# Transposing DMAs in place of TensorE transposes, and 111 instead of 105 tiles of the softmax on VectorE

## The chip, the cores and the metric

The kernel runs on one core of a Trainium2 chip. That core has a matrix engine (TensorE, "PE" in the profile), a vector engine (VectorE, "DVE"), a scalar engine that evaluates the exponential (ScalarE, "ACT"), a general engine (GpSimd, "POOL"), and a sequencer that mostly issues transfers (SyncE, "SP"). The engines run in parallel, each through its own list of instructions in a fixed order, and wait for one another through semaphores. An instruction that waits holds everything behind it on the same engine. The metric is the device time of one execution in microseconds (us); less is better.

## The reference

One input `x` of 2048 tokens by 512 features goes through two attention branches of 32 heads of width 16, and a gate per token mixes the two outputs:

```python
g = sigmoid((x * gate_w).sum(-1, keepdims=True))
# A: ordinary attention, no mask
q, k, v = heads(x @ A_wqkv)
a = concat(softmax(q @ k.T * 16 ** -0.5) @ v) @ A_wo
# B: linear attention with a learned feature map
q, k, v = heads(x @ B_wqkv)
phi = lambda u: concat(softmax(u @ w_phi), softmax(-u @ w_phi))   # 16 + 16 features
kv, z = phi(k).T @ v, phi(k).sum(tokens)
b = concat((phi(q) @ kv) / (phi(q) @ z + 1e-6)) @ B_wo
return g * a + (1 - g) * b
```

Everything that goes in or out is bfloat16. Branch A costs most by far: 32 heads times 2048 x 2048 scores, each of which needs an exponential.

## The kernel before

**Branch A.** The scores are cut into 2048 units of 128 keys by 512 queries. Four units (four heads, same keys and queries) make a pack, 16 packs (all keys) a group, and there are 32 groups: four chunks of 512 queries times eight groups of four heads. For a unit TensorE computes the scores (`_scores`, line 839), and most units get their exponential on ScalarE (`_exp`, line 891), three or two units in one instruction by turns, from a ring of five PSUM banks. The exponentiated tile then is the moving operand of the product with V (`_values`, line 958), and after the 16th pack of a group VectorE transposes and normalises the sums (`_norm`, lines 979 to 995).

**Packs away.** Some packs get their exponential on VectorE instead. `_vector_bits` (line 777, four instructions a pack) turns the scores into the bits of a bfloat16 power of two, and `_vector_terms` (line 795, three instructions a pack) makes three shifted copies. TensorE adds four such tiles with weights instead of one, so a pack away costs twelve more products. `PACKS` says how many packs of each group go away, `CHOICE` at which of the places 1, 4, 7, 10, 13 in the group: 105 packs in all.

**Branch B** is spread between the packs. `_b_fuse` folds `w_phi` into the weights of k and of q: it transposes a quarter of `WB` by TensorE against the identity (line 1050), copies it out of PSUM (line 1055), multiplies (line 1068, name `wphi`) and copies back (line 1073). `_b_pair` makes the features of two tiles of 128 tokens, with the exponential on ScalarE (line 1124). For queries, `_b_phit` transposes the features (TensorE line 1189, VectorE line 1196), `_b_num` forms numerator and denominator, divides, and transposes the result (lines 1235 and 1241), and `_b_out` multiplies by `WoB`. `_out` adds branch A's product, copies out of PSUM and stores.

**The start.** `x` is loaded in five pieces as it lies in memory and turned by TensorE (`_x_transpose`, line 609) and a copy on VectorE (line 615) into `xT`, the features on the partitions. The projections read `xT`. SP issues, in this order: the five pieces of `x`, three later parts of `A_wqkv`, `gate_w`, `B_wqkv`, the 32 small blocks of `w_phi`, the two output weights, and from then on only the stores.

**What sets the order.** A list scheduler in the kernel (`Plan.order`) writes the order of every engine at build time, by an account of costs and latencies written in the code (for instance 0.45 us of SP for each small transfer in `_shared_dma`, 0.5 for another one), by due times in packs (`prio`, `K0`, `SK`, `Q0`, `SQ`), release times (`rel`) and free PSUM banks. The order is then fixed: if a transfer lands later than that account has it, the engine waits at the instruction that needs it, however much other work stands behind. Scores have the first priority on TensorE, but they stand in the same single list.

## Time and profile before

| | us |
|---|---|
| median of three runs (lowest, highest) | 791.22 (790.95, 792.47) |
| time of the profiled execution | 790.92 |
| its span, which the trace covers | 788.9 |
| ScalarE busy | 768.6 |
| TensorE busy, as modelled | 766.6 |
| VectorE busy | 729.4 |

All three compute engines are busy for more than nine tenths of the span. The trace gives a start and an end to every instruction and tells what released it when its engine had been idle. A row of the table of instructions has the source line, the engine and operation, output and input tiles with shapes, the count, the total and mean time, and the idle time ahead of it with its cause. A row of the timeline has start, duration, engine and instruction; `SPq` is SP issuing a transfer, and the row covers the issuing alone, not the transfer.

### The profile page before, as it was taken

To read this page: it belongs to the slowest core of one execution; us is meant where nothing else is said; L and a number is where in the kernel's file an instruction comes from. 1 tells how busy PE (TensorE), PEld (TensorE's weight loads), DVE (VectorE), ACT (ScalarE), POOL (GpSimd) and SP (SyncE) were. 2 spreads that over 40 slices of the span, in tenths; PEclk is the share of its full clock that TensorE was granted. 3 is DMA by queue.
4 is the path that set the end of the run, shared out by engine and by line. 5 is a ranking of instruction groups with operands and counts; after the bars stand their busy time and mean duration, and the time that the engine had idled before them with its cause. 6 is when DMAs were issued, how large, how long until landed. Compare 5 with 4: busy or idle time off the path is not lost.

```text
span 788.9 us, 17147 instructions
## 1 busy us (share of the span) xinstructions
PE 766.6 (97%) x7506; PEld 243.9 (31%) x7506; DVE 729.4 (92%) x1325; ACT 768.6 (97%) x671; POOL 6.9 (1%) x14
## 2 busy tenths in 40 slices
PE   9999999999999999999999999999999999999998
PEld 4333333233222232222222333223332233223332
DVE  5778989898999999999999999899988999799994
ACT  5799999999999999999999999999999999999996
POOL 2000000000000000000000000000000000000000
PEclk9999999999999999999999999999999999999999
DMA  9200000000000000000000000000000000000000
GB/s 267 55 2 1 2 1 2 1 2 1 2 1 2 1 2 1 2 2 1 2 2 1 2 1 8 15 8 1 2 7 21 2 2 2 14 15 1 2 2 27
DMA packets 10857, 9.48 MB, mean 12 GB/s; under 512 B 3616, under 2 KB 10272, under 8 KB 10784
## 3 DMA queue, kind: packets, MB, share of 16 engines
q1 hardware_dynamic: 8912, 7.75, 3.2%
q8 instruction: 58, 0.95, 0.5%
q10 hardware_dynamic: 1872, 0.66, 0.3%
q14 instruction: 15, 0.12, 0.1%
HBM read 6.31 MB, written 2.10 MB: 11 GB/s over the span
## 4 chain that ended last, share of the span: by engine, by line
ACT 81%; DVE 9%; PE 9%; issue 0%
ACT ET L891 78%; ACT bq L1124 3%; DVE va L777 3%; PE ps L839 3%; DVE vp L795 2%; PE ps L958 2%; PE ps L634 1%; PE ps L688 1%; PE ps L1252 1%; PE ps L1285 0%; PE ps L594 0%; PE ps L965 0%; PE ps L609 0%; DVE xT L615 0%; DVE VB L1083 0%; DVE bq L1121 0%
## 5 line engine op out<-in xcount | busy, mean ns | idle before, releaser
L891 ACT ACTIVATE ET<-ps 128x1536 bf16<-128x1536 f32 (+1 forms) x651 | 740.5, 1327 | 11.4 <-PE ps L839 10.4
L839 PE MATMUL ps<-qT,kT 32*128 32x512 bf16 x2048 | 340.2, 384 | 12.7 <-ACT ET L891 8.7
L777 DVE TENSOR_SCALAR va<-ps 128x512 uint16<-128x512 f32 x420 | 276.5, 682 | 6.7 <-PE ps L839 5.9
L795 DVE TENSOR_SCALAR vp<-va 128x2048 uint16<-128x2048 uint16 x315 | 209.0, 686 | 1.3 <-PE ps L958 0.9
L839 PEld LDWEIGHTS ps<-qT,kT 32*128 32x128 bf16 x2048 | 83.9, 91 | 266.6 <-ACT ET L891 145.3
L958 PE MATMUL ps<-ET,V 128*32 128x512 bf16 x1628 | 158.4, 386 | 0.6 <-DVE T L979 0.3
L958 PE MATMUL ps<-vp,vc 128*32 128x512 bf16 x840 | 74.8, 384 | 0.9 <-DVE vp L795 0.9
L965 PE MATMUL ps<-kT,zero 128*32 128x512 bf16 x832 | 75.0, 386 | 0.0
L958 PEld LDWEIGHTS ps<-ET,V 128*32 128x32 bf16 x1628 | 41.3, 94 | 68.8 <-issue 57.0
L634 PE MATMUL ps<-WB,xT 128*128 128x512 bf16 x192 | 54.8, 383 | 0.6 <-DVE T L979 0.2
L958 PE MATMUL ps<-vp,V 128*32 128x512 bf16 x420 | 41.3, 384 | 0.9 <-DVE vp L795 0.9
L958 PE MATMUL ps<-va,V 128*32 128x512 bf16 x420 | 41.7, 387 | 0.0
L634 PE MATMUL ps<-xT,WA 128*128 128x512 bf16 (+1 forms) x132 | 36.8, 377 | 0.4 <-DVE va L777 0.2
L1124 ACT ACTIVATE bq<-bq 128x2048 bf16<-128x2048 bf16 x16 | 31.7, 1983 | 0.0
L958 PEld LDWEIGHTS ps<-vp,vc 128*32 128x32 bf16 x840 | 19.8, 95 | 34.3 <-issue 17.0
L965 PEld LDWEIGHTS ps<-kT,zero 128*32 128x32 bf16 x832 | 18.6, 94 | 36.2 <-issue 34.2
L979 DVE STREAM_TRANSPOSE T<-ps 128x512 f32<-128x512 f32 x32 | 22.7, 708 | 7.4 <-PE ps L958 7.3
L1099 DVE CAST bq<-ps 128x512 bf16<-128x512 f32 x32 | 21.8, 683 | 6.6 <-PE ps L634 6.6
L674 DVE TENSOR_TENSOR qT<-ps,mask 128x1024 bf16<-128x1024 f32 x15 | 18.3, 1217 | 2.8 <-PE ps L634 2.8
L634 PEld LDWEIGHTS ps<-WB,xT 128*128 128x128 bf16 x192 | 12.6, 97 | 24.8 <-issue 12.0
L1294 DVE CAST WB<-ps 128x512 bf16<-128x512 f32 x12 | 8.3, 690 | 12.6 <-PE ps L1285 11.2
L688 PE MATMUL ps<-WA,xT 128*128 128x128 bf16 x256 | 19.6, 220 | 0.0
(84 smaller groups left out, 439.6 us busy)
## 6 DMA issues: line engine op xcount, KB each, us to landing
xn<-in_A_x_dram SPq DMA_DIRECT2D x3, 512.0 KB, 7.1
WB<-in_B_wqkv_dram SPq DMA_DIRECT2D x1, 1536.0 KB, 8.8
out_dram<-WB SPq DMA_DIRECT2D x12, 128.0 KB, 1.7
WA<-in_A_wqkv_dram SPq DMA_DIRECT2D x3, 384.0 KB, 8.8
xn<-in_A_x_dram SPq DMA_DIRECT2D x2, 256.0 KB, 3.7
wphi<-in_B_w_phi_dram SPq DMA_DIRECT2D x32, 0.5 KB, 2.1
WoA<-in_A_wo_dram SPq DMA_DIRECT2D x1, 512.0 KB, 4.1
WoB<-in_B_wo_dram SPq DMA_DIRECT2D x1, 512.0 KB, 5.1
```

What stands on the lines that cost most here:

```text
L634: ins = e.matmul(self._bank(job)[:, 0:n], lhs(c), rhs(c), start=(c == 0), stop=(c == 3))
L674: [lambda e, b: e.tensor_tensor(self.qT[:, s0:s0 + 2, :], b[:, None, :].to_broadcast([P, 2, QCH]), self.mask[:, :, None].to_broadcast([P, ...
L688: ins = e.matmul(self._bank(job)[:, P * tt:P * tt + P], self.xT[:, c, QCH * j + TOK * tt:QCH * j + TOK * tt + TOK], self.WA[:, 2, c, P * c ...
L777: parts.append(op("DVE", lambda e, j=j, job=job: e.tensor_scalar(self.va[:, slot, j, :], self._bank(job), SCALE * LOG2E * 128.0, (127.0 - ...
L795: self.plan.op("DVE", lambda e, t=t, shift=shift: e.tensor_scalar(flat(t), a, float(shift), None, op0=ALU.add), 0.07 + n * 0.00026, reads= ...
L839: return e.matmul(out, self.kT[32 * i:32 * i + 32, cp, kt * TOK:(kt + 1) * TOK], self.qT[32 * i:32 * i + 32, s, :], start=True, stop=True, ...
L891: o = plan.op("ACT", lambda e: e.activation(self.ET[:, a % NS:a % NS + n, :], self.ps[:, self._ring(a):self._ring(a) + n, :], ACT.Exp, sca ...
L958: ins = e.matmul(self._bank(ot)[32 * i:32 * i + 32, :], V[:, v0:v0 + 32], tile, start=(kt == 0), stop=(kt == self.NT - 1), tile_position=( ...
L965: ins = e.matmul(self._bank(ot)[32 * i:32 * i + 32, :], self.zero[:], self.kT[:, 0, 0:QCH], start=False, stop=False, tile_position=(0, 32 ...
L979: op("DVE", lambda e: e.transpose(T1[:, side].rearrange("p b s -> p (b s)"), src()), 0.635, deps=last, writes=[b_T1[side]], name="n_t1", p ...
L1099: [lambda e, b, k=k: e.tensor_copy(bq[:, k].rearrange("p (g s v) -> p g s v", g=8, s=2)[:, :, 0, :], b.rearrange("p (g v) -> p g v", g=8))],
L1124: op("ACT", lambda e: e.activation(flat, flat, ACT.Exp), self.c_act(2048) + 0.045, reads=[b], writes=[b], name="b_exp", prio=due + 1)
```

## The change

All four kinds of transposes leave TensorE, with their copies on VectorE. A new helper `_turn` issues a transposing DMA from SP instead. `x` is turned straight from memory into `xT` in five such transfers (two of 256 tokens, three of 512), `WB` in eight (four for k, four for q, 128 x 512 each), the query features in 16 (128 x 1024) and the normalised output of branch B in 16 (128 x 512). The scheduler's account gives each 0.3 us of SP and 5.0 us (`TURN`) until the result is there; the three later pieces of `x` get 9 to 11.

`PACKS` and `CHOICE` become `AWAY`, five bits a group, with 111 packs away. By groups the counts are 1 2 4 4 3 3 2 2, 4 4 5 5 2 4 3 4, 5 1 4 4 5 4 4 1, 4 3 4 3 4 4 4 5; before they were 2 0 4 3 2 3 5 1, 5 4 3 3 5 5 4 2, 3 5 3 2 4 4 3 3, 2 5 2 3 3 5 4 3. Due times and lead times are set anew, and unused branches of the scheduler go. SP's order is unchanged up to the output weights; the transposes of `WB` stand behind those, and later the transposes of features and outputs stand between the stores.

```diff
-    NB, NVA, NVP, LEAD = 4, 4, 6, 11
-    FIRST = 6
+    NB, NVA, NVP, LEAD = 4, 4, 6, 12.75
+    FIRST = 5
...
-    KEEP, EARLY = 14, 2.5
+    KEEP = 14
+    TURN = 5.0
+    STEP, BITS, TERM, PVX, NORM, QDUE, PUT = 1.0, -80, 3.5, 0.65, -30, -15.5, 7.65
...
+        def load_x(j, lo, hi, lat):
+            self.b_xT[j].writers.append(self._turn(
+                f"x{lo}", self.xT[:, :, lo:hi], self.x2d[lo:hi, :], [], [], -50 + j, lat=lat))
...
-        load_x(0, [0], 4.0)
-        load_x(0, [1], 4.2)
+        for half in range(2):
+            load_x(0, QCH // 2 * half, QCH // 2 * (half + 1), self.TURN)
+            self.b_x0[half].writers = self.b_xT[0].writers[half:]
...
-        load_x(1, [0, 1], 8.0)
-        load_x(2, [0, 1], 9.0)
-        load_x(3, [0, 1], 10.0)
+        for j in range(1, self.NQC):
+            load_x(j, QCH * j, QCH * j + QCH, 8.0 + j)
...
-            for half in range(2):
-                mm = self._x_transpose(j, half, half if j == 0 else None)
-                if j == 0 and half == 0:
-                    self._warm(1, mm)
...
-    PACKS = (2, 0, 4, 3, 2, 3, 5, 1, 5, 4, 3, 3, 5, 5, 4, 2, 3, 5, 3, 2, 4, 4, 3, 3, 2, 5, 2, 3, 3, 5, 4, 3)
-    CHOICE = ((), (7,), (4, 10), (1, 7, 13), (1, 4, 10, 13), (1, 4, 7, 10, 13))
+
+    AWAY = (4, 17, 27, 23, 14, 21, 9, 9, 27, 15, 31, 31, 6, 15, 21, 27, 31, 8, 27, 29, 31, 15, 29, 8, 15, 21, 29, 13, 27, 30, 29, 31)
...
-    K0, SK, Q0, SQ = 30.0, 13.25, 226.0, 16.0
+    K0, SK, Q0, SQ = 19.0, 12.45, 221.0, 16.2
...
     def _b_fuse(self, s, due):
         op = self.plan.op
-        for half in range(2):
-            job = Job()
-            m = None
...
-                m = op("PE", tr, 4 * self.c_pe(128), reads=[self.b_WB, self.b_iden], deps=[m] + self.b_WT.readers,
-                       name="wtr", prio=due, rel=due - 10, acquire=None if c2 else job)
...
+        war = self.b_WT.readers
+        self.b_WT.writers, self.b_WT.readers = [self._turn(
+            f"wt{s}{c}", self.WT[:, :, P * c:P * c + P], self.WB[:, c, D * s:D * s + D], [self.b_WB], war, due, due - 10)
+            for c in range(4)], []
...
+    def _turn(self, name, out, src, reads, deps, due, rel=-99, lat=None):
+
+        return self.dma("SP", name, lambda e: e.dma_start_transpose(out, src), cost=0.3, reads=reads, deps=deps, prio=due,
+                        rel=rel, lat=lat or self.TURN)
+
+    def _b_phit(self, t, slot, k, due):
+        if t % 4 == 0:
             self.phit_war = list(self.b_phiT.readers)
             self.b_phiT.writers, self.b_phiT.readers = [], []
...
+        self.b_phiT.writers.append(self._turn(
+            f"ph{t}", self.phiT[:, :, t % 4 * TOK:t % 4 * TOK + TOK], self.bq[:, slot, k, :], [self.b_bq[slot]],
+            self.phit_war, due))
...
-        self.b_onTB.writers.append(op("DVE", lambda e: e.tensor_copy(
-            self.onTB[:, :, tt * TOK:tt * TOK + TOK],
-            self._bank(job).bitcast(BF16)[:, 0:D].rearrange("p (r q) -> p r q", q=TOK)), 0.34,
-            deps=[m] + self.ontb_war, name="nbt_ev", prio=due + 1, release=job))
+        self.b_onTB.writers.append(self._turn(
+            f"nb{t}", self.onTB[:, :, tt * TOK:tt * TOK + TOK], nb, [b_nb], self.ontb_war, due + 1))
```

## The prediction

> **What bounds the kernel now.** I read the page's busy shares and its chain of waits first, then the groups of instructions.

> ```profile
> PE 766.6 (97%) x7506; PEld 243.9 (31%) x7506; DVE 729.4 (92%) x1325; ACT 768.6 (97%) x671; POOL 6.9 (1%) x14
> ...
> ACT 81%; DVE 9%; PE 9%; issue 0%
> ...
> L891 ACT ACTIVATE ET<-ps 128x1536 bf16<-128x1536 f32 (+1 forms) x651 | 740.5, 1327 | 11.4 <-PE ps L839 10.4
> ...
> L777 DVE TENSOR_SCALAR va<-ps 128x512 uint16<-128x512 f32 x420 | 276.5, 682 | 6.7 <-PE ps L839 5.9
> L795 DVE TENSOR_SCALAR vp<-va 128x2048 uint16<-128x2048 uint16 x315 | 209.0, 686 | 1.3 <-PE ps L958 0.9
> ```

> Four fifths of the last chain is ScalarE, and line 891 idles 11.4 us in all. The timeline of ScalarE's first 40 us shows where:

> ```profile
> 9.36 18.24 ACT L891 ACTIVATE ET<-ps 128x1536 bf16<-128x1536 f32 x16 [5.70 <-PE ps L839]
> 30.62 2.36 ACT L891 ACTIVATE ET<-ps 128x1536 bf16<-128x1536 f32 x2 [3.02 <-PE ps L839]
> 34.61 6.03 ACT L891 ACTIVATE ET<-ps 128x1536 bf16<-128x1536 f32 x5 [1.63 <-PE ps L839]
> ```

> The first exponential starts at 9.36, 16 take 18.24 (1.14 each, 0.456 a unit, two and a half units each), then come two stalls of 4.65 together; the 21st starts at 34.61 + 2 x 1.18 = 37.0. After that ScalarE hardly stops. VectorE comes next (stretches of the span; columns: length, PE, PEld, DVE, ACT busy):

> ```profile
> 260.00:480.00 220.00, 213.98 (x2179) 63.04 (x2178) 219.12 (x403) 219.96 (x192) 0.00 (x0) 1.00 0.01 1
> 480.00:760.00 280.00, 272.78 (x2660) 83.73 (x2656) 261.80 (x487) 279.94 (x246) 0.00 (x0) 1.00 0.02 7
> ```

> To 480 us VectorE is as full as ScalarE; behind that it has 18 us to spare. Last, SP's timeline, on which the prediction hangs, and the transfers' landing times:

> ```profile
> 0.74 2.57 SPq L482 DMA_DIRECT2D xn<-in_A_x_dram  x5
> 3.35 4.57 SPq L487 DMA_DIRECT2D WA<-in_A_wqkv_dram  x3
> 7.96 3.11 SPq L502 DMA_DIRECT2D gw<-in_gate_w_dram  x4
> 11.11 0.44 SPq L504 DMA_DIRECT2D WB<-in_B_wqkv_dram  x1
> 11.59 16.96 SPq L541 DMA_DIRECT2D wphi<-in_B_w_phi_dram  x32
> 28.59 0.43 SPq L506 DMA_DIRECT2D WoA<-in_A_wo_dram  x1
> 29.06 0.51 SPq L508 DMA_DIRECT2D WoB<-in_B_wo_dram  x1
> ```

> ```profile
> out_dram<-WB SPq DMA_DIRECT2D x12, 128.0 KB, 1.7
> WA<-in_A_wqkv_dram SPq DMA_DIRECT2D x3, 384.0 KB, 8.8
> xn<-in_A_x_dram SPq DMA_DIRECT2D x2, 256.0 KB, 3.7
> ```

> SP issues without a pause to 29.57. The scheduler's account of the same list, with its new 0.3 for a piece of `x`, is 5 x 0.3 + 3 x 0.5 + 4 x 0.45 + 0.5 + 32 x 0.45 + 2 x 0.5 = 20.7: the order is written for a queue that is free 8.9 us earlier. So far nobody on TensorE felt that: line 1068 first runs at 45.1.

> **The change, part by part.**

> *Fewer units on ScalarE.* Six packs more go away: 24 units x 0.456 = -10.9 us. They cost VectorE 24 x 0.658 (276.5/420) + 18 x 0.663 (209.0/315) = 27.7.

> *Transposes gone.* VectorE loses the copies of lines 615, 1055, 1196 and 1241 (5.3 + 2.8 + 10.8 + 6.6 = 25.5), TensorE 288 matmuls (5.0 + 2.6 + 9.9 + 6.3 = 23.8); 72 products come for the packs away (72 x 0.089 = 6.4). VectorE is 2.2 us richer in work in a shorter span. TensorE is no bound, I count it nothing: scores go first and other work waits in its list.

> *Price of a transposing DMA.* The trace has none. To issue one: from 0.51 (2.57/5, `x`) to 1.52 (4.57/3, the slowest row). I take 1.52: in the built program it works in tiles of 16 rows by 128 columns, 32 to 128 of them, and so has more to generate than a load of rows. To land, from its issue: 1.7 to 8.8; I take 3.7, the unqueued transfer of 256 KB.

> *First score.* `x`'s second half lands at 0.74 + 1.52 + 3.7 = 6.0. Before, TensorE loaded the first weights of the queries' projection at 6.93, behind transposes and copies. Gain some 0.6 (from 1.1 to a loss of 2): start 8.8. Later pieces have slack: the last is issued at 6.8, and its keys were projected at 27.7 before.

> *The new wait.* In the changed order the first `wphi` product (line 1014 there) stands on TensorE directly behind the scores of the 20th exponential, and ahead of those of the 21st. It needs all four transposes of `WB`'s k part, and these stand on SP behind `WoB`. Free: 29.57 + 5 x (1.52 - 0.51) = 34.6. The fourth begins 3 x 1.52 later at 39.2 and lands at 42.9. One `wphi` (0.4), a set of values (0.4) and the scores (0.4) follow: the 21st exponential starts at about 44.2. ScalarE has finished its 20th at 8.8 + 22.8 = 31.6. So it stands 12.6 us; queued behind the waiting product is everything, also the scores for VectorE. The granted clock is 1.00 throughout this trace and TensorE never idle for so long, so whether its clock falls in such a stall can't be seen; I price that at nothing (0 to 2). The old stalls of 4.65 go. Net, the 21st starts 44.2 - 37.0 = +7.2 (from -2.9, with 0.51 and 1.7, to +20.8, with twice my prices).

> *The q part of `WB`.* Its transposes are issued when the last of the k products has read `WT`; the products that need it stand six score groups later (6 x 1.14 = 6.8), and they land after 3 x 1.52 + 3.7 = 8.3: +1.5 (0 to 7.5).

> *Features and outputs.* Here the account gives 5.3 from issue (5.6 for a pair); by my price a pair takes 1.52 + 3.7 = 5.2. Cover: the scheduler's other work. +0.5 (0 to 10, if the queue takes 3 us each).

> *VectorE.* Groups 18 to 31 carry 53 packs away instead of 46: 7 x 4.62 = +32.3, less some 14 of copies (12 of line 1196, 14 of 1241), in a stretch that ScalarE shortens by 7 x 1.82 = 12.8 and where 18 us were spare. Moving branch B's due times forward relieves it. +2 (0 to 12).

> *Tail.* The last group has 5 packs away: VectorE 23.1 us, ScalarE 11 x 1.82 = 20.1; before 13.9 and 23.7. Bits made ahead cover part: +2 (0 to 3).

> Sum: -10.9 + 7.2 + 1.5 + 0.5 + 2 + 2 = +2.3 on the profiled 790.92, whose span is 788.9: 793.2. The median shown, 791.22, is 0.3 above that execution; I say 793.

> [...]

> **Rivals.**

> 1. *Transposes issue like the loads they replace; faster.* At 0.51 and 3.7 the fourth part of `WB` lands at 29.57 + 1.53 + 3.7 = 34.8 and the 21st exponential starts at 36.1 (-0.9); the q part lands in 5.2, inside 6.8. Then -10.9 - 0.9 + 4 = -7.8: 783. For it: 0.51 is the row of the very loads replaced, and SP's slow `WA` rows (1.52) may only be backlog behind `x`. Against: tiles. It decides where 8 issues (five of `x`, three of `WB`) cost below about 1.3 each: there the delay eats no more than the gain.
> 2. *Twice my price (3 us to issue, 5.2 to land).* `WB` lands at 56.5: +20.8, q part +7.5, features some +10, the rest 4: +31, 822. For it only that nothing bounds it. [...]
> 3. *VectorE becomes the bound.* Forecast as it is, but nothing in groups 18 to 31 moves forward: +12 instead of +2, 803. For: no spare to 480 us. Against: due times of branch B move forward.

> **Chances.** Forecast (787 to 799) 0.47; rival 1 0.33; rival 2 0.10; rival 3 0.10. This kernel's runs tell no change from 0.2% (1.6 us). Rival 1 gives faster 0.30, same 0.03; the forecast, with a price near the break-even, faster 0.06, same 0.13, slower 0.28; the others slower 0.20. Together 0.36, 0.16, 0.48. The range leaves out the cheapest end of rival 1 and most of rival 2: 782 to 812; the forecast's own is 787 to 799.

> **What would show it.** Rows of SP: five transposes of `x` ending near 8.3, `WoB` near 34.6. A stall of ScalarE of 10 to 14 us behind its 20th exponential, the product at line 1014 released by a DMA; line 805 in 642 groups of exponentials' time 729.6. VectorE near 731. If the stall is under 5 us I am wrong on the price; if it is there and the time still falls, on VectorE or the tail; if ScalarE stalls after 400 us on `phiT` or `onTB`, the features' transposes cost more than taken.

## The result, and the profile after

The changed kernel takes 794.0 us in the median of 20 runs (790.7 to 800.6); the kernel before takes 791.1 (790.6 to 792.5). The ratio is 1.0046, with a 95% interval of 1.0030 to 1.0062: a little slower. The forecast was 793.0, and the wait that takes the gain back stands where the forecast had it. The profiled execution of the kernel after took 797.93 us with a span of 796.1, so it is one of the longer ones. The medians and ranges below leave out two slow single runs, over 1.5% above the fastest of their kernel: 805.7 us with the old spread, and 799.0 with `WB` turned by TensorE and eight loads.

From the profile page of the kernel after, the busy line, the chain of waits, the granted clock of TensorE in 40 slices, and the group of the exponential:

```profile
PE 749.2 (94%) x7248; PEld 233.9 (29%) x7314; DVE 729.8 (92%) x1323; ACT 758.9 (95%) x662; POOL 6.9 (1%) x14
...
PEclk9869999999999999999999999999999999999999
...
ACT 76%; PE 12%; DVE 6%; SPq 4%; issue 1%; DMA 0%; DVEq 0%
...
L853 ACT ACTIVATE ET<-ps 128x1536 bf16<-128x1536 f32 (+1 forms) x642 | 730.9, 1337 | 24.6 <-PE ps L805 21.9
```

ScalarE has 9.7 us less to do, as wanted, but waits 24.6 us instead of 11.4 at this line. SP's queue has come into the last chain with 4%, and the clock shows an 8 and a 6 in its second and third slices where there were only nines (a slice is 19.9 us). SP's timeline in the same kernel (start, duration of the issuing, transfer):

```profile
0.74 10.51 SPq L1130 DMA_TRANSPOSE xT<-in_A_x_dram  x5
11.29 1.72 SPq L488 DMA_DIRECT2D WA<-in_A_wqkv_dram  x3
13.05 2.48 SPq L503 DMA_DIRECT2D gw<-in_gate_w_dram  x4
15.57 0.43 SPq L505 DMA_DIRECT2D WB<-in_B_wqkv_dram  x1
16.05 17.43 SPq L542 DMA_DIRECT2D wphi<-in_B_w_phi_dram  x32
33.52 0.42 SPq L507 DMA_DIRECT2D WoA<-in_A_wo_dram  x1
33.98 0.51 SPq L509 DMA_DIRECT2D WoB<-in_B_wo_dram  x1
34.53 18.36 SPq L1130 DMA_TRANSPOSE WT<-WB  x8
```

The first transpose of `WB` is issued at 34.5. What waits for it, from the waits of TensorE (total, times, longest):

```profile
PE ps L1014 <- DMA WT<-WB: 10.6, 1, 10.6
```

One product of `_b_fuse` stands for 10.6 us. ScalarE's timeline shows what that does, and a second loss behind it (in brackets the idle time before the row):

```profile
25.27 7.15 ACT L853 ACTIVATE ET<-ps 128x1536 bf16<-128x1536 f32 x6 [0.29 <-PE ps L805]
43.15 1.45 ACT L853 ACTIVATE ET<-ps 128x1536 bf16<-128x1536 f32 x1 [10.73 <-PE ps L805]
45.19 1.02 ACT L853 ACTIVATE ET<-ps 128x1024 bf16<-128x1024 f32 x1 [0.59 <-PE ps L805]
46.71 1.45 ACT L853 ACTIVATE ET<-ps 128x1536 bf16<-128x1536 f32 x1 [0.49 <-PE ps L805]
48.33 1.02 ACT L853 ACTIVATE ET<-ps 128x1024 bf16<-128x1024 f32 x1 [0.17 <-PE ps L805]
50.27 1.45 ACT L853 ACTIVATE ET<-ps 128x1536 bf16<-128x1536 f32 x1 [0.92 <-PE ps L805]
53.17 1.02 ACT L853 ACTIVATE ET<-ps 128x1024 bf16<-128x1024 f32 x1 [1.45 <-PE ps L805]
```

Six exponentials take from 43.15 to 54.60, 11.45 us, where ScalarE by itself needs 6 x 1.14 = 6.84 (its first 14 took 15.97): another 4.6 us. Stretches of the same span tell why (length, PE, PEld, DVE, ACT, POOL busy, granted clock, DMA share, GB/s):

```profile
32.00:34.00 2.00, 0.00 (x0) 0.00 (x0) 0.00 (x0) 0.42 (x1) 0.00 (x0) 0.97 0.03 1
34.00:36.00 2.00, 0.00 (x0) 0.00 (x0) 0.00 (x0) 0.00 (x0) 1.31 (x1) 0.50 0.36 93
...
42.00:44.00 2.00, 2.00 (x14) 0.40 (x13) 0.69 (x1) 0.85 (x1) 0.00 (x0) 0.50 0.00 0
...
52.00:54.00 2.00, 2.00 (x11) 0.34 (x10) 0.99 (x2) 0.83 (x1) 0.00 (x0) 0.50 0.44 89
54.00:56.00 2.00, 2.00 (x14) 0.51 (x10) 1.46 (x3) 1.59 (x3) 0.00 (x0) 0.91 0.00 0
56.00:58.00 2.00, 2.00 (x25) 0.71 (x22) 1.71 (x4) 2.00 (x3) 0.00 (x0) 1.00 0.00 0
```

TensorE falls idle at 30.9, runs on half its clock from about 33.9 on (0.97 in the stretch from 32: half clock for the last 0.12 us of it), and stays there until about 54.4, though its work is back at 41.4. Up to 41.4 half speed costs nothing, since TensorE stands anyway; from there on TensorE sets the pace, and ScalarE waits for scores.

### The profile page after: what moved, and what is told of

Read it like the earlier page. It is cut to its first block, busy times and chain, and to the rows that moved or that the text cites. A ratio compares the mean times of both kernels' runs of the same rounds, so it can differ in the third digit from the quotient of the medians.

```text
span 796.1 us, 16743 instructions
## 1 busy us (share of the span) xinstructions
PE 749.2 (94%) x7248; PEld 233.9 (29%) x7314; DVE 729.8 (92%) x1323; ACT 758.9 (95%) x662; POOL 6.9 (1%) x14
## 2 busy tenths in 40 slices
DMA packets 47034, 16.83 MB, mean 21 GB/s; under 512 B 41840, under 2 KB 46448, under 8 KB 46960
## 4 chain that ended last, share of the span: by engine, by line
ACT 76%; PE 12%; DVE 6%; SPq 4%; issue 1%; DMA 0%; DVEq 0%
ACT ET L853 73%; PE ps L805 4%; PE ps L919 4%; ACT bq L1070 3%; DVE va L746 2%; SPq L542 2%; SPq L1130 2%; DVE vp L764 1%; PE ps L603 1%; PE ps L926 1%; PE ps L1181 1%; PE ps L1214 1%; DMA WT<-WB 0%; DVE kT L626 0%; SPq L503 0%
## 5 line engine op out<-in xcount | busy, mean ns | idle before, releaser
L853 ACT ACTIVATE ET<-ps 128x1536 bf16<-128x1536 f32 (+1 forms) x642 | 730.9, 1337 | 24.6 <-PE ps L805 21.9
L805 PE MATMUL ps<-qT,kT 32*128 32x512 bf16 x2048 | 343.6, 386 | 17.2 <-ACT ET L853 10.9
L746 DVE TENSOR_SCALAR va<-ps 128x512 uint16<-128x512 f32 x444 | 289.7, 679 | 9.9 <-PE ps L805 8.7
L764 DVE TENSOR_SCALAR vp<-va 128x2048 uint16<-128x2048 uint16 x333 | 219.7, 679 | 1.1 <-PE ps L919 0.8
L919 PE MATMUL ps<-ET,V 128*32 128x512 bf16 x1604 | 154.4, 389 | 0.6 <-DVE bq L1045 0.3
L919 PE MATMUL ps<-vp,vc 128*32 128x512 bf16 x888 | 80.1, 386 | 0.4 <-DVE vp L764 0.3
L603 PE MATMUL ps<-WB,xT 128*128 128x512 bf16 x169 | 50.8, 383 | 3.5 <-issue 1.9
L919 PE MATMUL ps<-va,V 128*32 128x512 bf16 x444 | 44.2, 389 | 0.0
L603 PE MATMUL ps<-xT,WA 128*128 128x512 bf16 (+1 forms) x113 | 32.9, 383 | 3.3 <-issue 1.8
L1070 ACT ACTIVATE bq<-bq 128x2048 bf16<-128x2048 bf16 x16 | 32.3, 2020 | 0.1
L926 PEld LDWEIGHTS ps<-kT,zero 128*32 128x32 bf16 x840 | 18.6, 94 | 31.6 <-issue 28.4
L1067 DVE TENSOR_TENSOR bq<-bq,btree 128x2048 bf16<-128x2048 bf16 x16 | 19.3, 1209 | 0.0
L1077 DVE TENSOR_TENSOR bq<-bq,brec 128x2048 bf16<-128x2048 bf16 x16 | 19.3, 1209 | 0.0
## 6 DMA issues: line engine op xcount, KB each, us to landing
out_dram<-WB SPq DMA_DIRECT2D x12, 128.0 KB, 1.7
WA<-in_A_wqkv_dram SPq DMA_DIRECT2D x3, 384.0 KB, 6.0
WA<-in_A_wqkv_dram ACTq DMA_DIRECT2D x3, 128.0 KB, 3.8
```

The costliest lines, as they stand in the source:

```text
L603: ins = e.matmul(self._bank(job)[:, 0:n], lhs(c), rhs(c), start=(c == 0), stop=(c == 3))
L746: parts.append(op("DVE", lambda e, j=j, job=job: e.tensor_scalar(self.va[:, slot, j, :], self._bank(job), SCALE * LOG2E * 128.0, (127.0 - ...
L764: self.plan.op("DVE", lambda e, t=t, shift=shift: e.tensor_scalar(flat(t), a, float(shift), None, op0=ALU.add), 0.07 + n * 0.00026, reads= ...
L805: return e.matmul(out, self.kT[32 * i:32 * i + 32, cp, kt * TOK:(kt + 1) * TOK], self.qT[32 * i:32 * i + 32, s, :], start=True, stop=True, ...
L853: o = plan.op("ACT", lambda e: e.activation(self.ET[:, a % NS:a % NS + n, :], self.ps[:, self._ring(a):self._ring(a) + n, :], ACT.Exp, sca ...
L919: ins = e.matmul(self._bank(ot)[32 * i:32 * i + 32, :], V[:, v0:v0 + 32], tile, start=(kt == 0), stop=(kt == self.NT - 1), tile_position=( ...
```

## The experiments

The theory: the change as such gains some ten microseconds, and one transfer that comes late takes them back, in two ways, by the wait itself and by the slow TensorE behind it. What makes it late is SP's queue: five dearer transposes of `x` and, ahead of the transposes of `WB`, 32 small loads of `w_phi`. Rivals: the wait costs nothing that the slow clock does not cost; the price is the scheduler's wrong account in general, not this transfer; one of the four moved transposes, or the new spread of packs, is itself a loss.

### TensorE kept busy while it waits

46 sets of four products with zeros (they add nothing) stand in TensorE's list ahead of the first product that needs `WT`. They fill TensorE from 30.7 to 40.8 us, and the last transpose lands at 40.5.

```diff
+            q = p.queues["PE"]
+            at = next(i for i, o in enumerate(q) if o.name == "wphi")
+            def busy(e):
+                for _ in range(46):
+                    ins = self._fill(e, self.ot[0])
+                return ins
+            q.insert(at, Op("PE", busy, 9.8, "busy", 0.0, -99, "col", 0.2))
```

> The changed kernel with 46 sets of products with zeros (each adds nothing to the open sums; 46 x 0.2133 = 9.8 us by the kernel's own figure) put on TensorE directly ahead of the first wphi product, so that TensorE is busy for nearly all of the time in which it waited for the transposes of WB. My theory: the wait itself stays (21st exponential still near 43 us, since the transposes land at 41.1), and the slow stretch behind it (granted clock 0.53 from 43 to 55 us, 4.6 us lost over six exponentials) comes from the clock that fell during the idle time, so it goes: about 4.5 us below the changed kernel, 789 to 790. Rival: the slow stretch is work that piled up behind the wait (keys' projections, wphi, gate); then it stays and the time stays at 794.

Measured: 796.9 us (794.9 to 797.4, four runs), ratio 1.0064 (1.0046 to 1.0082). Two lines of this kernel, one of ScalarE's timeline and one of the stretches:

```profile
42.06 10.68 ACT L861 ACTIVATE ET<-ps 128x1536 bf16<-128x1536 f32 x9 [9.75 <-PE ps L813]
```

```profile
43.00:55.00 12.00, 10.70 (x97) 3.64 (x95) 9.41 (x15) 10.75 (x10) 0.00 (x0) 0.93 0.32 46
```

ScalarE's wait stays (9.75), and the slow stretch right behind it is gone: nine exponentials follow each other without a gap, and the clock is full until 53.4. So the slow stretch was TensorE's clock, which at this place fell with TensorE idle (0.50 from 34 us on) and did not with TensorE busy (1.00 from 32 to 43 us, busy for 10.83 of the 11). The 0.93 of the line comes from 3.4 us at half clock from 53.4 on, behind a product's wait of 1.17 for the q part of `WT` (one of its four issues took 2.36 us). The forecast of the time failed. Against the profiled execution after, 5.0 us are won in the wait and the six exponentials; two waits at 53.5 and 55.6 take back 1.9, and three short falls of the clock near 384, 468 and 748 us cost 3.4 (waits of 1.2, 0.8 and 1.4) where the kernel after has one of 0.9. That is 0.6 us won, and the span is 0.6 shorter (795.5 against 796.1). Why all four runs lie above 794, where the fastest of the kernel after take 791, stays open.

### The loads of w_phi in eight, and steps between

`w_phi` comes in eight transfers of four blocks instead of 32 of one. The scheduler still counts 14.4 us for them, so the order of all other engines' instructions is that of the kernel after.

```diff
-        for c in range(4):
-            for hh in range(8):
-                parts.append(lambda e, c=c, hh=hh: e.dma_start(
-                    self.wphi[16 * hh:16 * hh + 16, c, 16 * hh:16 * hh + 16], self.B_w_phi[8 * c + hh, :, :]))
+        W8 = self.B_w_phi.rearrange("(c g) p j -> g p c j", g=8)
+        for hh in range(8):
+            parts.append(lambda e, hh=hh: e.dma_start(
+                self.wphi[16 * hh:16 * hh + 16, :, 16 * hh:16 * hh + 16], W8[hh]))
...
-        self._shared_dma("wphi", parts, b := B(), -5, [z])
+        self._shared_dma("wphi", parts, b := B(), -5, [z], 14.4)
```

> The changed kernel with the 32 small loads of w_phi issued as 8 of four blocks each; all engines but SP keep their order. SP should reach the transposes of WB some 13 us earlier (24 issues at 0.54), limited by WB's own landing at about 23 us, so they land near 30 us, where TensorE comes to the first wphi product at 31. My theory (the loss is the queue of SP, and the clock behind it): the stall of 10.7 us and the slow stretch of 4.6 go, 794 - 15 = 779, and the granted clock is near 1. Rival (the new DMAs or VectorE cost the gain later): the stall goes, but the time stays above 787.

Measured: 781.25 us (780.9 to 782.3), ratio 0.9877 (0.9862 to 0.9892): faster than both kernels. Its timelines of SP and of ScalarE:

```profile
15.06 4.82 SPq L542 DMA_DIRECT2D wphi<-in_B_w_phi_dram  x8
...
22.85 17.63 SPq L1130 DMA_TRANSPOSE WT<-WB  x8
```

```profile
28.00 26.43 ACT L853 ACTIVATE ET<-ps 128x1536 bf16<-128x1536 f32 x23 [0.52 <-PE ps L805]
```

The transposes start 11.7 us earlier (SP is free for them at 20.9 and then waits for `WB` itself), no wait of TensorE on a DMA is left there, and ScalarE runs through. Nothing else was touched, so the long queue costs the kernel after all of its difference to this one: 12.7 us in the median. The fastest runs of the two are 9.8 us apart (790.7 and 780.9), about the wait alone.

In two further kernels the loads are 16 (two blocks each, below) and 24 (the pieces are (0, 2), (2, 3), (3, 4)), with the same account and order.

```diff
+            for lo, hi in ((0, 2), (2, 4)):
+                parts.append(lambda e, hh=hh, lo=lo, hi=hi: e.dma_start(
+                    self.wphi[16 * hh:16 * hh + 16, lo:hi, 16 * hh:16 * hh + 16], W8[hh, :, lo:hi]))
```

> As with w_phi in 8 loads, but in 16 (two blocks each); the orders of all engines but SP stay. SP comes to the transposes of WB at about 25.2 us (8 issues of 0.54 later than with 8), the fourth lands near 31.6, TensorE comes there at 31.0: a stall of ScalarE of 0 to 2 us. If a late transpose costs what it is late and nothing else, 782 to 784; the granted clock stays near 0.999.

> As before it, with 24 loads. SP comes to the transposes of WB near 29.6 us, the fourth lands near 36: a stall of 5 to 6 us. If lateness alone counts, 781.25 + 5.5 = 787. If TensorE's clock falls in the stall and stays low behind it, as behind the stall of 10.7 us of the changed kernel, some 2 to 5 us more (789 to 792), with a granted clock of 0.99 and a slow stretch behind the stall.

The four kernels side by side; wait and half-speed time are those of the profiled execution, the time at half speed worked out from its stretches of 2 us. Against the kernel before, 16 loads give 0.9971 (0.9940 to 1.0001) and 24 loads 1.0015 (0.9991 to 1.0040), in ten runs each:

| loads of w_phi | wait of ScalarE behind its 20th exponential | half speed from about 33 us on | median us | fastest and slowest us, with mean clock |
|---|---|---|---|---|
| 8 | none (0.5 at most) | none | 781.25 | 780.9 (0.999), 782.3 (0.997) |
| 16 | 2.36 | 17.1 us | 789.7 | 783.2 (0.999), 793.7 (0.982) |
| 24 | 5.18 | 6.8 us | 791.8 | 789.3 (0.991), 796.6 (0.982) |
| 32 (after) | 10.73 | 20.5 us | 794.0 | 790.7 (0.992), 800.6 (0.978) |

The wait grows with the number of loads; the time does not grow in step with it. Lateness alone would put 16 loads some 2 us above 8, and that is what its fastest run shows (783.2 at a clock of 0.999); its slowest is 10.5 us longer with the same program. The profiled execution of 16 loads has a wait of 2.2 us on TensorE and then half clock until about 49.5:

```profile
34.71 1.45 ACT L854 ACTIVATE ET<-ps 128x1536 bf16<-128x1536 f32 x1 [2.36 <-PE ps L806]
36.76 1.02 ACT L854 ACTIVATE ET<-ps 128x1024 bf16<-128x1024 f32 x1 [0.59 <-PE ps L806]
...
44.73 1.02 ACT L854 ACTIVATE ET<-ps 128x1024 bf16<-128x1024 f32 x1 [1.46 <-PE ps L806]
```

With 24 loads TensorE waits longer, 5.0 us, but half clock is over sooner, at 40.6. I had expected 782 to 784 for 16 loads, which fails in the median: here the clock fell in a wait of 2.2 us already, and stayed at half for 17.1 us, against 6.8 behind the wait of 5.0. The 789 to 792 expected for 24 loads with a slow clock came, but not for the reason given: behind the wait of 5.18 half clock costs only 0.9 us in the profiled execution, and three short falls of the clock near 377, 462 and 742 us cost 3.4. The same three cost 3.4 with 16 loads; with eight the profiled execution has none.

### The scheduler's account as measured

The account is put right, and the scheduler writes a new order: 1.26 us of SP for a transpose and 2.0 until it lands, 1.3 to 2.6 us for a piece of `x`, 0.55 for a small load. The loads of `w_phi` stay 32.

```diff
-    TURN = 5.0
+    TURN = 2.0
...
-        return self.dma("SP", name, lambda e: e.dma_start_transpose(out, src), cost=0.3, reads=reads, deps=deps, prio=due,
+        return self.dma("SP", name, lambda e: e.dma_start_transpose(out, src), cost=cost, reads=reads, deps=deps, prio=due,
...
-        o = self.plan.op("SP", parts, 0.45 * len(parts), name="dma_" + name, prio=prio, deps=deps, lat=8.0)
+        o = self.plan.op("SP", parts, 0.55 * len(parts), name="dma_" + name, prio=prio, deps=deps, lat=8.0)
```

> The changed kernel, with the scheduler's account of SP and of the transposing DMAs set to what the trace shows (1.26 us to issue a transpose of WB, of features or outputs, 1.3 and 2.6 for the pieces of x, 0.55 for a small load; 2.0 from then to landing, 3 for x). SP's list stays, the order of the other engines is written anew, so that wphi stands where its transposes land. My theory: no stall over 2 us behind the 20th exponential, 779 to 785 (the order differs everywhere, so a few us either way). Rival (a late wphi delays all of branch B and VectorE cannot make it up): no stall, but 788 or more.

Measured: 788.8 us (786.8 to 793.7, ten runs), ratio 0.9978 (0.9953 to 1.0003). SP's queue is as long as in the kernel after (the transposes of `WB` start at 33.8), but the wait is gone, since other work now stands ahead of the product:

```profile
25.43 37.87 ACT L853 ACTIVATE ET<-ps 128x1536 bf16<-128x1536 f32 x33 [0.29 <-PE ps L805]
```

So a late transfer that the order knows of does not stop TensorE. The gain of 5 is smaller than the 9 to 15 expected. The time fits the rival named beforehand (a late `wphi` delays all of branch B): ScalarE waits between 80 and 200 us instead (7.2 in five pieces). That the late start of branch B is the cause was not shown, since the whole order is new. The same account with eight loads:

> w_phi in 8 loads, and the scheduler's account of SP and of the transposing DMAs set to the measured issue and landing times (0.55 for each of the 8). Candidate for the fastest: no wait for a transpose is left in either account, so against the kernel with w_phi in 8 loads (781.25) I expect 776 to 785; if the accounts mattered only through that one wait, the two agree within 3 us. Rival (every new order costs some, as the true account with 32 loads did, 788.8): 785 to 789.

Measured: 782.1 us (781.0 to 786.2), ratio 0.9894 (0.9866 to 0.9922), the same as with eight loads and the old account. Where the transfer is in time the wrong account does no harm.

### Is a part of the change itself a loss?

Each of these starts from the kernel with eight loads (781.25), in which nothing is late, and undoes one part; the scheduler then writes a new order. First the old spread of 105 packs:

```diff
-    AWAY = (4, 17, 27, 23, 14, 21, 9, 9, 27, 15, 31, 31, 6, 15, 21, 27, 31, 8, 27, 29, 31, 15, 29, 8, 15, 21, 29, 13, 27, 30, 29, 31)
+    PACKS = (2, 0, 4, 3, 2, 3, 5, 1, 5, 4, 3, 3, 5, 5, 4, 2, 3, 5, 3, 2, 4, 4, 3, 3, 2, 5, 2, 3, 3, 5, 4, 3)
+    CHOICE = ((), (7,), (4, 10), (1, 7, 13), (1, 4, 10, 13), (1, 4, 7, 10, 13))
```

> As the kernel with w_phi in 8 loads, but with the old 105 packs away at the old places (PACKS, CHOICE). 24 units more on ScalarE at 0.456: if the six packs are worth what the prediction counted (10.9 less 2 for VectorE and 2 for the tail), this is 7 to 11 us slower than that kernel, near 788. If the spread is worth nothing because VectorE binds, the two agree within 2 us.

Measured: 789.1 us (788.3 to 794.0, six runs), ratio 0.9982 (0.9961 to 1.0003). The six packs are worth 7.8 us, inside what was expected: ScalarE's busy time goes from 757.9 to 769.6, and the wait at the end of the span from 6.4 back to 3.7. Then `x` loaded as it lies and turned by TensorE, as before the change:

```diff
-            self.b_xT[j].writers.append(self._turn(
-                f"x{lo}", self.xT[:, :, lo:hi], self.x2d[lo:hi, :], [], [], -50 + j, lat=lat))
+                self.dma("SP", f"x{j}{h}", lambda e, t0=t0, t1=t1: e.dma_start(self.xn[:, t0:t1, :], x4[:, t0:t1, :]),
+                         writes=[self.b_xn[j][i] for i in halves], prio=-50 + j, lat=lat)
...
+                mm = self._x_transpose(j, half, half if j == 0 else None)
```

> w_phi in 8 loads, but x loaded as it lies and turned by TensorE and VectorE as before; all other transposes by DMA. SP is free some 8 us earlier, VectorE gets 5.3 us of copies in the first 30 us. If x by DMA is worth what its place says (the start 0.4 us, the two old stalls of ScalarE between 27 and 35 us of 4.65), this is 3 to 6 us slower than 781.25: 784 to 787. If x by DMA is worth nothing, within 1.5 us of it.

Measured: 792.2 us (791.0 to 794.7), ratio 1.0012 (0.9999 to 1.0024), 11 us more than with the transposing DMAs and well above what I expected. The first exponential starts at 10.09 instead of 8.86, there are waits of 0.9 and 1.9 at 24 and 33, and 6.9 us in five waits from 100 to 151 us. That last part, far from the pieces of `x`, I put down to the order that the scheduler then writes; if so, 11 is the price of this kernel, not of the operation. Features and outputs turned by TensorE, with copies on VectorE:

```diff
-        self.b_phiT.writers.append(self._turn(
-            f"ph{t}", self.phiT[:, :, t % 4 * TOK:t % 4 * TOK + TOK], self.bq[:, slot, k, :], [self.b_bq[slot]],
-            self.phit_war, due))
+        m = op("PE", tr, 8 * self.c_pe(128), reads=[self.b_bq[slot], self.b_iden], deps=self.phit_war, name="phit",
+               prio=due, acquire=job)
+        o = op("DVE", lambda e: e.tensor_copy(
...
```

> w_phi in 8 loads, with the query features and branch B's output turned by TensorE and copied by VectorE as before (x and WB by DMA). VectorE gets 10.8 + 6.6 = 17.4 us of copies, nearly all behind 390 us, where the kernel with 111 packs leaves it some 20 us. If VectorE has become the bound there, 8 to 16 us slower than 781.25: 789 to 797, with idle ScalarE behind 400 us. If its spare time takes them, within 3 us.

Measured: 797.9 us (796.9 to 801.0), ratio 1.0091 (1.0067 to 1.0115), 16.7 us more, just above the range. VectorE has 746.5 us of work instead of 730.8, and the end of the span waits for it: it works on the last packs without a pause from 769.9 to 786.5, where ScalarE has been done since 777. The waits of ScalarE in this kernel:

```profile
ACT xT L1242 <- PE ps L1236: 16.3, 1, 16.3
ACT ET L853 <- PE ps L805: 12.4, 7, 5.7
```

With 111 packs away VectorE has no room for these copies: the spread needs the transposing DMAs of features and outputs. Last, the transposes of `WB` back on TensorE, once with 32 loads of `w_phi` and once with eight; `_b_fuse` is that of the kernel before:

```diff
-        self.b_WT.writers, self.b_WT.readers = [self._turn(
-            f"wt{s}{c}", self.WT[:, :, P * c:P * c + P], self.WB[:, c, D * s:D * s + D], [self.b_WB], war, due, due - 10)
-            for c in range(4)], []
+                        ins = e.transpose(bank[:, 512 * c2 + P * cp:512 * c2 + P * cp + P],
+                                          self.WB[:, c, D * s + P * cp:D * s + P * cp + P], self.iden[:])
+            o = op("DVE", lambda e, half=half, job=job: e.tensor_copy(
...
```

> The transposes of WB alone go back to TensorE and VectorE as before the change; x, features and outputs stay with the transposing DMAs, the 32 loads of w_phi too. The first product of WB's k part stays at its place in TensorE's list, but now needs only the loads of w_phi and the copies out of PSUM. My theory (what costs is where the result comes late, which is SP's queue of 32 small loads with the transposes behind it): the last load of w_phi is issued near 33.0 and lands near 34.8, so TensorE waits from about 31.5 to 34.8 and ScalarE stands 3 to 4 us there instead of 10.7; 784 to 788 where the clock holds, up to 793 where it falls behind the wait as with 16 loads. If the wait has nothing to do with the loss: 793 or more. If transposing WB by DMA was itself worth something in the rest of the kernel (VectorE has four more copies of 0.62 us): some 2 us above that.

> Both at once: w_phi in 8 loads and WB turned by TensorE. No wait of TensorE on a DMA is left between 20 and 60 us. If the transposing DMAs of WB do no harm when they are in time, nor much good, this takes what the kernel with 8 loads takes, 781 to 783; if they relieve VectorE where it is full, 784 to 786; if they disturb something when in time, under 780.

Measured: 794.5 us (794.1 to 795.9), ratio 1.0047 (1.0034 to 1.0060), with 32 loads; 787.8 (786.8 to 796.4, 11 runs), ratio 0.9987 (0.9960 to 1.0014), with eight. The local reading holds. With 32 loads the wait is 3.59, inside the 3 to 4 expected, and now for `w_phi` itself; with eight it is 1.06. The totals come out high: 794.5 is at the very top of what was expected, with a fallen clock and a worth of the transposing DMAs themselves, and 787.8 is above the 784 to 786. By its number alone 794.5 could also mean that the wait has nothing to do with the loss; the 6.7 us that eight loads save here too speak against that. Both have waits of about 6 us between 110 and 185 us, 3.2 of them at one instruction of branch B that waits for VectorE. ScalarE's timeline with eight loads:

```profile
110.99 1.91 ACT L1085 ACTIVATE bq<-bq 128x2048 bf16<-128x2048 bf16 x1 [3.22 <-DVE bq L1082]
141.60 4.62 ACT L853 ACTIVATE ET<-ps 128x1536 bf16<-128x1536 f32 x4 [1.55 <-PE ps L919]
```

With transposing DMAs and eight loads there are 2.2 us of waits in that stretch. VectorE is busy 39.5 of the 40 us from 120 to 160, against 38.3 with transposing DMAs. So the transposing DMAs of `WB`, in time, are worth some 6.5 us in this kernel (787.8 against 781.25); they are not the loss, their lateness is. How much of it is the four copies (0.69 each in the kernel before, where 0.62 was expected) and how much the changed order was not separated.

### The packs of the last group

The last group has three packs away instead of five (109 in all), to shorten the end.

```diff
-29, 31)
+29, 21)
```

> w_phi in 8 loads, with three packs away in the last group instead of five (109 in all). ScalarE gets 8 units, 3.6 us; the wait for the last output copy (6.44 us, 3.68 before the change) should fall by the 2.8 us that the two packs were thought to cost the tail. So within 1.5 us of 781.25. If the tail does not depend on the last group, 784.5 to 785.5.

Measured: 784.6 us (783.2 to 787.9), ratio 0.9929 (0.9905 to 0.9952). The wait at the end shrinks from 6.4 to 3.8, as expected. The time does not stay within 1.5 us, as it was to; it is 3.4 longer: two packs more on ScalarE (3.6 us), and in the profiled execution two short falls of the clock near 455 and 735 us with 2.1 us of waits. The spread with 111 packs stays the better one.

## Why the prediction was right, and where its sum was off

Against its own time of 790.92 the sum gave +2.3; the profiled execution after is 7.0 longer, the median of all runs 2.9 longer.

- **Fewer units on ScalarE**, -10.9: the busy time of the exponentials fell by 9.6 (740.5 to 730.9). With nothing late, the six packs were worth 7.8 net, with what they cost at the end of the span.
- **The price of a transposing DMA**, 1.52 to issue and 3.7 to land: measured for a quarter of `WB` 1.27 and 2.6, for the features 1.32 and 3.2, for the outputs 1.19 and 2.4, for the pieces of `x` 1.3 to 3.1 and 4.7 (medians of the listing by line and of the DMA issues). Too dear by a fifth for `WB`, too cheap for `x`. Packets under 512 bytes went from 3616 before to 41840 after; that issuing is dearer on their account, or for the tiles, no run shows. That `WB` was to be issued from 34.6, and was from 34.5, is luck: the pieces of `x` took 10.51 instead of the 7.6 counted, and the rows of `WA`, counted at their old 4.57, took 1.72. The slow rows of `WA`, which set my price, were thus not what issuing costs; the first rival's reading as backlog fits: without plain loads of `x` ahead of them they take 0.57 each. The fourth quarter landed at 41.1 instead of 42.9. And the bound of +20.8, "twice my prices", has only the issuing doubled, and 5.2 to land; with 7.4 it is 23.0.
- **The first score** at 8.8: 9.0.
- **The new wait**, 12.6 at the 21st exponential, which was to start 7.2 later: 10.73, and 6.2 later. It is the product named, released by the transfer named, and the old waits of 4.65 are gone as said.
- **TensorE's clock**, priced at nothing (0 to 2): 4.6 us behind this wait alone in the profiled execution, and the spread of 10 us among the runs. This is the step that was mis-sized. That the trace of before had no such idle stretch was a reason to widen the range, not to take the lower end.
- **The q part**, +1.5, and **features and outputs**, +0.5: neither is seen as a wait of its own in the kernel after. For the q part, half speed delayed its reader there; but with eight loads and a full clock there is no wait either, since its four transposes land 6.4 us after the first is issued (35.35 to 41.73), inside the cover of 6.8, and not after 8.3. The wait of 1.17 came where TensorE was kept busy and one issue took 2.36.
- **VectorE**, +2: ScalarE's waits behind 60 us, without the end, are 3.4 against 0.8 before, so +2.6. But all of them are for TensorE: the largest, 1.94 at 152 us, for a product of line 919, and 0.9 at 470 for scores at a short fall of the clock. The size fits; that VectorE is the cause is not shown. Its busy time is 729.8, near the 731 forecast.
- **The end**, +2: 6.44 instead of 3.68, +2.8.

From these, -9.6 + 6.2 + 4.6 + 2.6 + 2.8 = +6.6, against a span that grew by 7.2. Without what the clock cost (4.6, and 0.9 at 470 us) the list gives +1.1 where the sum had +2.3. So the forecast was a little too high without the clock and left the clock out; that the median of runs between 790.7 and 800.6 lies 1.0 from it is partly luck.

Of the rivals, the first (transposes issue like loads, 783) falls by its own condition: eight issues below 1.3 us each were wanted, and they are three of about 1.25 and five of 2.1 on the average. Its outcome, a faster kernel without the delay, is what the kernel with eight loads shows (781.25), but by another way: a quarter of `WB` still takes 1.27 to issue, and fewer issues stand ahead of it. The second rival (822) and the third (VectorE as the bound, 803) did not come; VectorE came close, as the copies put back on it show.

## What to carry to other kernels

Before a load is turned into a transposing DMA, count what its queue has to issue ahead of it, small transfers above all: here 32 loads of 512 bytes cost 17 us of issuing, and making them eight was worth 12.7 us, where the whole change had lost 2.9. Issuing the transposes ahead of the small loads was not tried; `w_phi`, which the same products read, would then be the later one. Where a list is fixed at build time, an operation whose result may come late should have other work ahead of it, or a true account. And a wait on TensorE is to be priced with the slow clock that may follow: here that cost 4.6 us behind a wait of 10.73 and 0.9 behind one of 5.18, and the mean clock of one program differed from run to run (0.978 to 0.992).

## What the runs showed of the hardware

**3.4 us at half clock cost about 1.4 us, as an estimate.** Over the 20 runs of the kernel after, time and mean granted clock go together (correlation -0.98, 0.65 us for 0.001). 3.4 us at half speed lower the mean over 790 us by 3.4 x 0.5 / 790 = 0.0022, and the runs' clocks (0.978, 0.980, 0.982, 0.984, 0.986, 0.989, 0.990, 0.992) lie mostly about that far apart. So by this estimate the spread of 10 us among runs of one program is six or seven times 3.4 us at half clock. The 20 runs of the kernel before lie within 1.9 us.

**Short falls far from any long wait.** In the profiled execution of the kernel after there is one fall of 3.4 us near 469 us (0.92 and 0.65 in two stretches of 4 us), others near 380, 460 and 745 us in other kernels (with 24 loads 0.96 in each of the three stretches of 40 us that hold them). Ahead of the one near 469 TensorE has less to do for a moment: from 464 to 468 its records fill 2.33 us of four, with 18 matmuls against 53 in the four before. That is not the whole of it: with the measured account the clock falls near 718 for about twice as long (0.97 from 680 to 720 us, 0.94 from 720 to 760), where the records fill 39.70 of the 40 us from 680 to 720. And no late transfer is needed: with eight loads and the measured account, where TensorE waits for no transfer behind the start, the clock falls near 454 (0.99 from 400 to 600 us).

**Issuing a transposing DMA** took 1.19 to 1.32 us (medians) for 128 x 512 and 128 x 1024 from SBUF, with single ones of 2.2, and 1.3 to 3.1 for the pieces of `x` from DRAM. A transfer of one 512-byte block of `w_phi` took 0.54, one of four blocks 0.60.
